# All of GpSimd's transfers kept in program order, and the token tiles of the mixer's second stage loaded two tiles ahead

## The chip, the cores and the metric

The kernel runs on one core of a Trainium2 chip. The core has five engines that run side by side, each with an in-order queue of its own: TensorE (PE in the profile, with its weight loads as PEld), VectorE (DVE), ScalarE (ACT), GpSimd (POOL) and SyncE (SP, which here only issues transfers). Transfers between HBM and on-chip memory are issued from an engine's queue and carried out by 16 DMA engines that all queues share. An engine waits for another, or for a transfer, through semaphores. The metric is the device time of one execution in microseconds, as the median over runs.

## The reference

The program has two halves that meet at the end. With `xn` the layer norm of the input `x` (2048 tokens by 512):

```
q = xn @ wq                        # 32 heads of 128
p = softmax(q k^T / sqrt(128))     # cached k, v: 32 heads x 2048 x 128
s = (p v) @ wo

h  = gelu(layernorm(xn) @ w1)      # 512 x 512
hs = shift(h) @ w2                 # four column groups, shifted by +1, -1, +2, -2 tokens
x1 = xn + hs
h2 = gelu(layernorm(x1) @ w3) @ w4 # 512 x 1792, 1792 x 512
g  = silu(x1 + h2)

out = x + s * g
```

The second half is called the mixer here. Inputs and output are bf16; sums are in fp32.

## The kernel before

The tokens are cut into 16 tiles of 128 (`t`), and into 4 groups of 512 (`qt`). The attention half is a sequence of 128 units: 8 groups of 4 heads, times 4 token groups, times 4 heads. A unit has 8 slots, 1024 slots in all. In each slot PE computes two blocks of scores (`ps_s`), ACT takes their exponential (`pT`, line 207), and PE multiplies an earlier slot's exponentials by the values (`ps_o`). VectorE adds up the exponentials (`acc`, lines 213 to 223).

The sums reach the normalisation by way of transfers on SP's queue: a transpose of `acc` (line 255), a sum and a reciprocal on VectorE (`sm`, `rc`, lines 260 and 245), a store of 2 KB to DRAM (`dr`, line 247), a broadcast load (`rb`, line 277), and then the product `oT = ps_o * rb` on VectorE (line 287). It reads a `ps_o` bank, of which there are two. The output projection collects four heads in `ps_wo`, and VectorE adds that to `s_acc` (line 361), after which the bank is free. The query projection of the unit after next (`ps_q`) uses the same bank.

The mixer's matmuls are pieces of work between these slots. A deque holds chunks, and each unit takes some five matmuls from it:

- Stage 1, `m1_chunk`: 16 chunks of 4 matmuls, GELU, result `hT`.
- Stage 2, `m2_chunk(t)`: 16 chunks of 4 matmuls, one per token tile, about 173 to 300 us. Tile `t` of the input is loaded as `xr` (`xn_load`, line 566), normalised in place on VectorE (`norm1`, line 411) when the chunk begins, and gets half of `ps_m` added (line 583). That is x1, which is stored to DRAM (`x1_d`, called `x_d` in the trace, line 585). Its statistics follow on VectorE (lines 589 and 590) and a reciprocal root on GpSimd (lines 127 and 128).
- Stage 3, `m3_chunk(c, fc)`: for each of 4 token groups (passes) 14 chunks of 4 matmuls with w3. `ln2` reloads four x1 tiles (`x1r`, line 613), normalises them eight slots later (line 620) and transposes them through SP (`xn2T`, line 623). The w3 weights come in pairs of chunks on GpSimd's queue (`w_sb`, line 657), each into one of two buffers when PE is done with it; w4 is loaded once (line 605).
- Stage 4, `m4_chunk(t)`: for each tile of the pass 14 matmuls with w4. x1 is loaded again as `xr` (line 667), `ps_m` is added (line 675), and after a tanh the gate `g` is stored to DRAM (`g_d`, lines 683 and 685).

In the last head group the output is made: for each tile `fin_load` loads `x` and `g` (`xl`, `gl`, lines 350 and 352), and `wo_out` computes the product and the sum (lines 366 and 368) and stores them (line 369). The last four tiles take another way, with loads on SP (`gf`, `xf`, lines 324 and 326).

Two pools of token tiles matter for the change: tag `tb` with 4 buffers holds `xr`, and tag `ta` with 6 buffers holds `x1r`, `xl` and `gl` (and earlier the input of the first layer norm).

What sets the order: nearly every instruction is wrapped in `pin`, which is `tc.keep_in_program_order`. Pinned instructions of an engine stay in the order in which the code writes them. An instruction that isn't pinned is placed by a scheduler, which can move it ahead of pinned ones on its engine's queue. Before the change these were free: `xl` and `gl`, the stage-2 store of x1, the reloads `x1r`, the stage-4 load of x1, and the store of `g`. All are transfers on GpSimd's queue. The loads of the w3 and w4 weights, of the stage-2 token tiles and GpSimd's arithmetic were pinned.

Of the kernel before, what the change touches and what calls it, by code (L numbers as in the profile page):

```python
# [11 lines left out]
BF16 = mybir.dt.bfloat16  # L12
# [5 lines left out]
def kernel(  # L18
# [15 lines left out]
    nc = tc.nc  # L34
    P = nc.NUM_PARTITIONS
# [3 lines left out]
    Sq, D = x2d.shape  # L39
# [4 lines left out]
    NT = Sq // P  # L44
# [18 lines left out]
    pin = tc.keep_in_program_order  # L63

    def pool(name, bufs=1, space=None, **kw):
        if space is not None:
            kw["space"] = space
        return tc.tile_pool(name=name, bufs=bufs, **kw)
# [16 lines left out]
        out=ident[:], in0=diag[:], scalar1=0.0, scalar2=None, op0=ALU.is_equal))  # L85
# [13 lines left out]
    tokp = ent(pool("tok", 4))  # L99
# [7 lines left out]
    xsrc = x2d.rearrange("(t p) d -> t p d", p=P)  # L107
    wq_v = A_wq.rearrange("(dc p) j -> p dc j", p=P)
    w3_v = B_w3.rearrange("(dc p) f -> p dc f", p=P)
    x1_d = [dsp.tile([P, D], BF16, name=f"x1_d{t}") for t in range(NT)]  # L110
    o_d = {qt: dsp.tile([P, HG, 512], BF16, name=f"o_d{qt}") for qt in range(QT)}
    g_d = [dsp.tile([P, D], BF16, name=f"g_d{t}") for t in range(NT)]
# [8 lines left out]
    def mm(out, lhsT, rhs, start, stop):  # L121
        mm_count[0] += out.shape[-1] / 512
        pin(nc.tensor.matmul(out=out, lhsT=lhsT, rhs=rhs, start=start, stop=stop))  # L123

    def rsqrt(out, var):
        ve = smp.tile([P, 1], FP32, name="ve")
        pin(nc.gpsimd.tensor_scalar(out=ve[:], in0=var, scalar1=EPS, scalar2=None, op0=ALU.add))
        pin(nc.gpsimd.tensor_tensor(out=out, in0=ve[:], in1=nhalf[:, 0:1], op=ALU.pow))
# [13 lines left out]
    def at(n, fn):  # L142
        todo[n].append(fn)

    def soft(n):
        while n % SPU not in (3, 5, 7):
            n += 1
        return n

    def evict(n):  # L150
        return n if n % SPU == SPU - 1 else n + 1
# [195 lines left out]

    def fin_load(t):
        xl = tokp.tile([P, D], BF16, tag="ta", bufs=6, name="xl")
        nc.gpsimd.dma_start(out=xl[:], in_=xsrc[t])  # L350
        gl = tokp.tile([P, D], BF16, tag="ta", bufs=6, name="gl")
        nc.gpsimd.dma_start(out=gl[:], in_=g_d[t][:])
        fin[t] = (xl, gl)

    def wo_post(g, t):
# [54 lines left out]
    def norm1(t, out, in_):  # L410
        pin(nc.vector.tensor_scalar(
            out=out, in0=in_, scalar1=mv1[t][:, 0:1], scalar2=rs1[t][:],
            op0=ALU.subtract, op1=ALU.mult))
# [70 lines left out]
    mlp = {}  # L484
# [70 lines left out]
    def m1_chunk(tt, jc):  # L555
        b = BASE_J[jc]
        jp = jc // 2
        return gelu_chunk(
            lambda dc: w1_sb[:, dc, jc * P:(jc + 1) * P],
            lambda dc: xnT[:, dc, tt * 512:(tt + 1) * 512],  # L560
            jc % 2, None,
            lambda: hT[:, 2 * jp:2 * jp + 2, b + tt * 512: b + (tt + 1) * 512])

    def xn_load(t):
        mlp["xnext"] = tokp.tile([P, D], BF16, tag="tb", bufs=4, name="xr")
        pin(nc.gpsimd.dma_start(out=mlp["xnext"][:], in_=xsrc[t]))

    def m2_chunk(t):
        def run(i, n):
            if i == 0:  # L570
                mlp["stage"] = 2
                mlp["ps"] = psX.tile([P, 512], FP32, tag="xm", name="ps_m")
                xr = mlp["xr"] = mlp.pop("xnext")
                at(n + 1 if n % SPU == 2 else n, lambda: norm1(t, xr[:], xr[:]))
                if t + 1 < NT:
                    xn_load(t + 1)
            c0 = BASE_J[i] + t * P - SHIFT[i]
            mm(mlp["ps"][:], hT[:, i, c0:c0 + P], w2_sb[:, i, :], i == 0, i == DC - 1)
            if i == DC - 1:
                ps, xr = mlp["ps"], mlp["xr"]  # L580

                def x1():
                    pin(nc.vector.scalar_tensor_tensor(
                        out=xr[:], in0=ps[:], scalar=0.5, in1=xr[:], op0=ALU.mult, op1=ALU.add))
                    nc.gpsimd.dma_start(out=x1_d[t][:], in_=xr[:])

                def stats():
                    bn = smp.tile([P, nc.vector.BN_STATS_DIM], FP32, name="bn")
                    pin(nc.vector.bn_stats(out=bn[:], in_=xr[:]))
                    pin(nc.vector.bn_aggr(out=mv2[:, t, :], in_=bn[:]))  # L590
                    rsqrt(rstd2[:, t:t + 1], mv2[:, t, 1:2])

                at(evict(n), x1)
                at(soft(n + 2), stats)
        run.size = DC
        return run
# [10 lines left out]
    def ln2(c, n):  # L607
        def start():
            mlp["xn2T"] = mp.tile([P, DC, 512], BF16, name="xn2T")
            xs = []  # L610
            for ts in range(4):
                xr = tokp.tile([P, D], BF16, tag="ta", bufs=6, name="x1r")
                nc.gpsimd.dma_start(out=xr[:], in_=x1_d[c * 4 + ts][:])
                xs.append(xr)
            mlp["xs"] = xs

        def apply(ts):
            t = c * 4 + ts
            xr = mlp["xs"][ts]
            pin(nc.vector.tensor_scalar(  # L620
                out=xr[:], in0=xr[:], scalar1=mv2[:, t, 0:1], scalar2=rstd2[:, t:t + 1],
                op0=ALU.subtract, op1=ALU.mult))
            pin(nc.sync.dma_start_transpose(
                out=mlp["xn2T"][:, :, ts * P:(ts + 1) * P], in_=xr[:]))

        at(n, start)
        for ts in range(4):
            at(soft(n + 8 + 2 * ts), lambda ts=ts: apply(ts))
# [31 lines left out]
    def m4_chunk(t):  # L660
        ts = t % 4

        def run(i, n):
            if i == 0:
                mlp["ps"] = psX.tile([P, 512], FP32, tag="xm", name="ps_m")
                mlp["xr"] = tokp.tile([P, D], BF16, tag="tb", bufs=4, name="xr")
                nc.gpsimd.dma_start(out=mlp["xr"][:], in_=x1_d[t][:])
            mm(mlp["ps"][:], mlp["h2"][i // 2][:, i % 2, ts * P:(ts + 1) * P],
               mlp["w4"][i][:], i == 0, i == FC - 1)
            if i == FC - 1:  # L670
                ps, xr = mlp["ps"], mlp["xr"]
                th = tokp.tile([P, D], BF16, tag="th", bufs=1, name="th")

                def x2():
                    pin(nc.vector.scalar_tensor_tensor(
                        out=xr[:], in0=ps[:], scalar=0.5, in1=xr[:], op0=ALU.mult, op1=ALU.add))

                def tanh(n):
                    pin(nc.scalar.activation(out=th[:], in_=xr[:], func=ACT.Tanh, scale=0.5))
                    at(soft(n + 2), silu)  # L680

                def silu():
                    pin(nc.vector.scalar_tensor_tensor(  # L683
                        out=xr[:], in0=th[:], scalar=1.0, in1=xr[:], op0=ALU.add, op1=ALU.mult))
                    nc.gpsimd.dma_start(out=g_d[t][:], in_=xr[:])  # L685

                at(evict(n), x2)
                at(n + 3, lambda: act_late.append(tanh))
        run.size = FC
        return run  # L690

    chunks = deque()
    hooks = {}
    for tt in range(QT):
        for jc in range(DC):
            chunks.append(m1_chunk(tt, jc))
    hooks[len(chunks) - 1] = lambda n: xn_load(0)
    for t in range(NT):
        if t == 8:
            hooks[len(chunks)] = lambda n: ln2(0, n)  # L700
# [78 lines left out]
    def normed(u):  # L779
        norm(u)  # L780
        gg, qq, hh = units[u]
        if hh == HG - 1 and (gg, qq) in deferred:
            pin(nc.sync.dma_start(out=o_d[qq][:], in_=oTs[(gg, qq)][:]))
        elif hh == HG - 1:
            wo_todo.extend((gg, 4 * qq + ts) for ts in range(4))
            if gg == NG - 1:
                fin_load(4 * qq)

    for n in range(NS):
# [46 lines left out]
        if p == 6 and wo_box:  # L836
            gg, t = wo_todo.popleft()
            wo_post(gg, t)
            if gg == NG - 1:
                at(n + 5, lambda t=t: wo_out(t))  # L840
                if t % 4 < 3:
                    fin_load(t + 1)
        if u == QUIET - 1 and p >= 6:
            wo_mm(*wo_todo[0], (0, 1) if p == 6 else (2, 3), "xm")
            if p == 7:
                gg, t = wo_todo.popleft()
# [47 lines left out]
    ts = [4 * LQ + j for j in range(4)]  # L894
# [75 lines left out]
```

## Time and profile before

| | us |
|---|---|
| median of 3 runs | 1255.7 (1254.87, 1255.70, 1258.52) |
| the profiled execution | 1254.97 |
| its span in the trace | 1253.2 |
| PE busy in the span | 1236.1 |
| ACT busy | 1129.9 |
| DVE busy | 1107.3 |
| POOL busy | 139.4 |

"Busy" leaves out instructions that only issue transfers on SP, set registers or wait. The span is what the trace covers; the rest of the profiled execution's time lies around it. In lists of waits a row names the engine that waited, its instruction, whom it waited for, the total, the number and the longest. In a timeline each row has the start, the duration, the engine, the line, the operation, the tile written and the tiles read, and in brackets the idle time before it and who ended it. PE's own durations overlap, as matmuls are pipelined: the distance of two starts is the better measure there. Some matmul records are missing in the trace.

The times of transfers from issue to landing, as medians in the view of transfers: `xr` from the input 2.4 us, `x1r` 3.5, `xr` from x1 2.6, `xl` 3.9, `gl` 2.9 (all 128 KB), w3's `w_sb` 3.8 (256 KB), `rb` 4.0 (256 KB), `dr` 1.7 (2 KB). The mean rate over the span is 101 GB/s, that of the fastest of the 40 slices 181. In 240 to 300 us the 16 transfer engines were busy for 0.62 of the time, in 405 to 450 for 0.59, in 620 to 665 for 0.67 and in 840 to 885 for 0.45.

### The profile page before, as it was taken

The page shows a single profiled execution, that of the slowest core. Times are in us where ns is not written, and L with a number is a line of the kernel's source. Part 1 is how long each engine was busy: PE and PEld are TensorE (multiplying, and loading weights), DVE is VectorE, ACT ScalarE, POOL GpSimd, SP SyncE. Part 2 cuts the span into 40 slices and gives each one's busy share as a digit, 9 for nine tenths or more (in the row PEclk, how much of TensorE's full clock was granted, in tenths as well). Part 3 has the DMA queues.
Part 4 walks back from the last instruction along what each step waited for, and adds up shares of the span by engine and source line. Part 5 has one row for each costly group of instructions (what it writes and reads, how often), then busy time and mean ns, then how long its engine had stood idle before and what let it go on. Part 6 is the DMA issues. An engine that isn't in the chain of part 4 may idle for free.

```text
span 1253.2 us, 16467 instructions
## 1 busy us (share of the span) xinstructions
PE 1236.1 (99%) x5757; PEld 597.9 (48%) x5872; DVE 1107.3 (88%) x1509; ACT 1129.9 (90%) x1285; POOL 139.4 (11%) x239
## 2 busy tenths in 40 slices
PE   8999999999999999999999999999999999999998
PEld 5444444444444444444444444444444444444444
DVE  7999999989899988889988889898888899888887
ACT  8999998888999888899988889998888999998893
POOL 4410013343101000000000000000000000000111
PEclk9999999999999999999999999999999999999999
DMA  9654453475635555344564345544446343552532
GB/s 181 140 111 93 79 111 89 115 151 135 129 75 112 108 101 104 62 96 90 103 120 72 77 101 97 106 72 100 99 89 114 67 81 81 117 116 55 151 77 68
DMA packets 235108, 126.70 MB, mean 101 GB/s; under 512 B 186832, under 2 KB 212048, under 8 KB 235024
## 3 DMA queue, kind: packets, MB, share of 16 engines
q1 hardware_dynamic: 225920, 100.40, 40.2%
q0 software_dynamic: 8672, 24.91, 7.9%
q8 instruction: 46, 0.75, 0.3%
q14 instruction: 38, 0.31, 0.1%
q10 hardware_dynamic: 432, 0.33, 0.1%
HBM read 82.58 MB, written 7.60 MB: 72 GB/s over the span
## 4 chain that ended last, share of the span: by engine, by line
PE 92%; DVE 3%; DMA 2%; ACT 1%; issue 1%; SPq 0%; POOL 0%; DVEq 0%; POOLq 0%
PE ps_o L123 33%; PE ps_s L123 33%; PE ps_m L123 9%; PE ps_q L123 8%; PE ps_wo L123 8%; ACT pT L207 1%; DVE acc L218 1%; DMA dr<-rc 1%; DMA xn2T<-x1r 0%; DVE oT L287 0%; DMA xr<-in_A_x_dram 0%; DMA vb<-in_A_v_cache_dram 0%; DVE acc L213 0%; SPq L158 0%; DMA rb<-dr 0%
## 5 line engine op out<-in xcount | busy, mean ns | idle before, releaser
L207 ACT ACTIVATE pT<-ps_s 128x1024 bf16<-128x1024 f32 x1024 | 1023.8, 1028 | 101.8 <-PE ps_s L123 87.4
L123 PE MATMUL ps_o<-pT,vb 128*128 128x512 bf16 x2014 | 600.6, 379 | 4.6 <-DVE oT L287 0.6
L123 PE MATMUL ps_s<-qT,kT 128*128 128x512 bf16 x1992 | 596.9, 379 | 2.3 <-ACT pT L207 0.5
L123 PEld LDWEIGHTS <-kT 128*128 128x128 bf16 x2048 | 231.0, 113 | 226.4 <-issue 4.9
L218 DVE TENSOR_TENSOR acc<-acc,pT 128x2048 bf16<-128x2048 bf16 x254 | 306.6, 1207 | 10.1 <-ACT pT L207 9.9
L123 PEld LDWEIGHTS <-vb 128*128 128x128 bf16 x2048 | 200.0, 98 | 226.6 <-issue 1.5
L213 DVE TENSOR_TENSOR acc<-pT 128x2048 bf16<-128x2048 bf16 x128 | 156.2, 1220 | 32.0 <-ACT pT L207 31.6
L123 PE MATMUL ps_q<-xnT,wq_h 128*128 128x512 bf16 (+1 forms) x516 | 151.0, 374 | 2.4 <-DVE s_acc L361 1.4
L123 PE MATMUL ps_wo<-wo_h,oT 128*128 128x512 bf16 (+1 forms) x470 | 138.8, 377 | 0.3
L287 DVE TENSOR_TENSOR oT<-ps_o,rb 128x512 bf16<-128x512 f32 x114 | 122.2, 1072 | 9.5 <-DMA rb<-dr 9.4
L361 DVE TENSOR_TENSOR s_acc<-ps_wo,s_acc 128x512 f32<-128x512 f32 x100 | 68.8, 688 | 43.8 <-PE ps_wo L123 42.9
L222 DVE TENSOR_TENSOR acc<-acc 128x1024 bf16<-128x1024 bf16 x127 | 86.8, 684 | 0.9
L193 DVE CAST qT<-ps_q 128x512 bf16<-128x512 f32 x109 | 75.0, 688 | 8.1 <-PE ps_q L123 7.4
L123 PEld LDWEIGHTS <-wq_h 128*128 128x128 bf16 x524 | 50.8, 98 | 62.5 <-issue 2.9
L260 DVE TENSOR_REDUCE sm<-accT 128x4 f32<-128x512 bf16 x114 | 77.5, 679 | 0.0
L123 PE MATMUL ps_m<-w_sb,h2T 128*128 128x512 bf16 x221 | 75.9, 379 | 0.1
L123 PE MATMUL ps_m<-xn2T,w_sb 128*128 128x512 bf16 x219 | 75.7, 379 | 0.1
L123 PEld LDWEIGHTS <-oT 128*128 128x128 bf16 x484 | 47.3, 98 | 56.5 <-DVE oT L294 0.6
L657 POOL DMA_DIRECT2D w_sb<-in_B_w_dram x28 | 21.1, 753 | 331.4 <-PE ps_m L123 273.5
L223 DVE TENSOR_TENSOR acc<-acc 128x512 bf16<-128x512 bf16 x127 | 54.0, 425 | 4.4
L685 POOL DMA_DIRECT2D g_d<-xr x16 | 8.8, 547 | 348.3 <-DVE xr L683 348.3
L496 DVE SCALAR_TENSOR_TENSOR sq<-sq,pre 128x1024 bf16<-128x1024 bf16 x36 | 44.0, 1222 | 4.0 <-ACT sq L492 4.0
(89 smaller groups left out, 599.8 us busy)
## 6 DMA issues: line engine op xcount, KB each, us to landing
rb<-dr SPq DMA_DIRECT2D x128, 256.0 KB, 4.0
vb<-in_A_v_cache_dram SPq DMA_DIRECT2D x64, 256.0 KB, 3.6
w_sb<-in_B_w_dram POOLq DMA_DIRECT2D x28, 256.0 KB, 3.8
wo_h<-in_A_wo_dram SPq DMA_DIRECT2D x32, 128.0 KB, 2.9
wq_h<-in_A_wq_dram SPq DMA_DIRECT2D x28, 128.0 KB, 2.9
kT<-in_A_k_cache_dram SPq DMA_TRANSPOSE x128, 3.4
dr<-rc SPq DMA_DIRECT2D x128, 2.0 KB, 1.7
xr<-in_A_x_dram POOLq DMA_DIRECT2D x16, 128.0 KB, 2.4
```

Source lines behind the costliest of these rows:

```text
L123: pin(nc.tensor.matmul(out=out, lhsT=lhsT, rhs=rhs, start=start, stop=stop))
L193: pin(nc.vector.tensor_copy(out=qT[:], in_=st[u].pop("psq")[:]))
L207: pin(nc.scalar.activation(out=s["pT"][-1][:, jj:jj + 2, :], in_=sps[:], func=ACT.Exp, scale=SCALE))
L213: pin(nc.vector.tensor_tensor(out=s["acc"][:], in0=s["pT"][0][:], in1=s["pT"][1][:], op=ALU.add))
L218: pin(nc.vector.tensor_tensor(out=a[:], in0=a[:], in1=st[u]["pT"][i][:], op=ALU.add))
L222: pin(nc.vector.tensor_tensor(out=a[:, 0:2, :], in0=a[:, 0:2, :], in1=a[:, 2:4, :], op=ALU.add))
L223: pin(nc.vector.tensor_tensor(out=a[:, 0, :], in0=a[:, 0, :], in1=a[:, 1, :], op=ALU.add))
L260: pin(nc.vector.tensor_reduce(out=sm[:], in_=s.pop("at")[:], axis=mybir.AxisListType.X, op=ALU.add))
L287: pin(nc.vector.tensor_tensor(out=oTs[(g, qt)][:, hh, :].rearrange(f, j=4), in0=s["o"].rearrange(f, j=4), in1=s["rb"].rearrange("x (p j) - ...
L361: pin(nc.vector.tensor_tensor(out=sa, in0=ps[:], in1=sa, op=ALU.add))
L496: pin(nc.vector.scalar_tensor_tensor(out=sq[:].rearrange(f2), in0=sq[:].rearrange(f2), scalar=1.0, in1=pre[:].rearrange(f2), op0=ALU.add, ...
L657: pin(nc.gpsimd.dma_start(out=w[:], in_=w3_v[:, :, fc * P:(fc + 2) * P]))
```

## The change

Two things are changed. First, the free transfers on GpSimd's queue are pinned: all of that queue is now in the order of the code. Second, the stage-2 token tiles are loaded two tiles ahead rather than one: a deque `xq` takes the place of the single name `xnext`, two tiles are loaded before the stage begins, and chunk `t` loads tile `t + 2`.

```
@@ fin_load
-        nc.gpsimd.dma_start(out=xl[:], in_=xsrc[t])
+        pin(nc.gpsimd.dma_start(out=xl[:], in_=xsrc[t]))
-        nc.gpsimd.dma_start(out=gl[:], in_=g_d[t][:])
+        pin(nc.gpsimd.dma_start(out=gl[:], in_=g_d[t][:]))
@@ xn_load
+    xq = deque()
     def xn_load(t):
-        mlp["xnext"] = tokp.tile([P, D], BF16, tag="tb", bufs=4, name="xr")
-        pin(nc.gpsimd.dma_start(out=mlp["xnext"][:], in_=xsrc[t]))
+        xq.append(tokp.tile([P, D], BF16, tag="tb", bufs=4, name="xr"))
+        pin(nc.gpsimd.dma_start(out=xq[-1][:], in_=xsrc[t]))
@@ m2_chunk
-                xr = mlp["xr"] = mlp.pop("xnext")
+                xr = mlp["xr"] = xq.popleft()
                 at(n + 1 if n % SPU == 2 else n, lambda: norm1(t, xr[:], xr[:]))
-                if t + 1 < NT:
-                    xn_load(t + 1)
+                if t + 2 < NT:
+                    xn_load(t + 2)
...
-                    nc.gpsimd.dma_start(out=x1_d[t][:], in_=xr[:])
+                    pin(nc.gpsimd.dma_start(out=x1_d[t][:], in_=xr[:]))
@@ ln2, start
-                nc.gpsimd.dma_start(out=xr[:], in_=x1_d[c * 4 + ts][:])
+                pin(nc.gpsimd.dma_start(out=xr[:], in_=x1_d[c * 4 + ts][:]))
@@ m4_chunk
-                nc.gpsimd.dma_start(out=mlp["xr"][:], in_=x1_d[t][:])
+                pin(nc.gpsimd.dma_start(out=mlp["xr"][:], in_=x1_d[t][:]))
...
-                    nc.gpsimd.dma_start(out=g_d[t][:], in_=xr[:])
+                    pin(nc.gpsimd.dma_start(out=g_d[t][:], in_=xr[:]))
@@ the list of chunks
-    hooks[len(chunks) - 1] = lambda n: xn_load(0)
+    hooks[len(chunks) - 1] = lambda n: [xn_load(t) for t in range(2)]
```

## The prediction

> **What bounds the kernel now.** I read the page's busy shares and 40 slices first, then PE's waits, then the timeline where PE stood still, then the transfers' times.
>
> ```profile
> PE 1236.1 (99%) x5757; PEld 597.9 (48%) x5872; DVE 1107.3 (88%) x1509; ACT 1129.9 (90%) x1285; POOL 139.4 (11%) x239
> PE   8999999999999999999999999999999999999998
> ```
>
> TensorE is full from end to end, at a mean granted clock of 0.999. Inside the steady work a 512-column matmul starts every 0.216 us (pairs 0.43 apart). So only time in which PE stands still can be won, and GpSimd (POOL), whose queue this change reorders, is at 11%. The list of PE's waits says how much that is:
>
> ```profile
> engine line waited for: us in total, times, longest us
> PE ps_q L123 <- DVE s_acc L361: 1.4, 1, 1.4
> PE ps_s L123 <- DVE ident L84: 1.4, 1, 1.4
> PE ps_o L123 <- DVE oT L287: 0.6, 2, 0.4
> ```
>
> The `ident` row is the start of the program. The first row and half of the third are one event. The timeline from 258 to 277 us shows it (start, duration, engine, line, what; in brackets the idle time before and who ended it):
>
> ```profile
> 258.22 0.55 POOL L613 DMA_DIRECT2D x1r<-x_d  x1 [3.25 <-DVE x1r L620]
> ...
> 260.18 0.54 POOL L585 DMA_DIRECT2D x_d<-xr  x1 [1.41 <-DVE xr L583]
> ...
> 265.82 0.55 POOL L613 DMA_DIRECT2D x1r<-x_d  x1 [5.10 <-DMA xn2T<-x1r]
> ...
> 267.69 0.62 POOL L566 DMA_DIRECT2D xr<-in_A_x_dram  x1
> ...
> 271.70 0.41 DVE L411 TENSOR_SCALAR xr<-xr,mv,rs 128x512 bf16<-128x512 bf16 x1 [3.13 <-DMA xr<-in_A_x_dram]
> 271.85 0.59 PE L123 MATMUL ps_o<-pT,vb 128*128 128x512 bf16 x2
> ...
> 273.90 0.59 PE L123 MATMUL ps_q<-xnT,wq_h 128*128 128x512 bf16 x2 [1.45 <-DVE s_acc L361]
> ...
> 275.49 1.05 DVE L287 TENSOR_TENSOR oT<-ps_o,rb 128x512 bf16<-128x512 f32 x1
> ...
> 276.60 0.59 PE L123 MATMUL ps_o<-pT,vb 128*128 128x512 bf16 x2 [0.38 <-DVE oT L287]
> ```
>
> The reader is to see a chain over four engines. An x1 reload (L613), which the scheduler had moved far ahead, sits on POOL's in-order queue and waits 5.10 us for a buffer that a transposing DMA still reads. Behind it stands the load of token tile 12 (L566, 267.69), only one tile ahead of its use. VectorE's normalisation L411 waits 3.13 us for that load, and everything behind it on VectorE is late: L361, which frees the bank that the next `ps_q` needs, and then L287, which frees a `ps_o`. PE's gaps: 271.85 to 273.90 is 2.05 us for two matmuls of 0.216, so 1.62 us lost; 275.62 to 276.60 is 0.98, so 0.55 lost. Together 2.17 us.
>
> Two smaller losses I found by the same sum over PE's starts: 0.41 us before 442.12 (L287 waited 2.66 us for its `rb`) and 0.37 us around 655 to 657 (L287 had waited 1.38 us). After the first 100 us PE loses nothing else: 2.95 us in all.
>
> **The change part by part.**
>
> *No instruction is added or removed.* In the two programs' instruction lists PE, ACT, DVE and SP have the same instructions in the same order; only POOL's order differs. POOL's transfers cost 0.54 to 0.63 us of its time each (0.75 for w3), as before.
>
> *Token loads two ahead (L566), the stage-2 x1 stores (L585) in order.* In the new POOL order the load of tile 12 stands after the store of tile 9 and its two small rsqrt operations, some 252 us, with no reload before it that waits for a buffer. With the median 2.4 us of its row it lands by 255, 16 us before L411 wants it. Of the four `tb` buffers a load takes the one of four tiles earlier, whose store is two tiles old. Nothing is late next on that path: the other 15 L411 show no wait even with loads one tile ahead. Worth: minus 2.17 us.
>
> *The x1 reloads (L613) in order.* They no longer float one by one into stages 2 and 4, but go in four groups of four, where the code writes them: the first at about 234 us, the others behind the last w3 load of a pass (405.26, 624.09, 842.90), each with a token or x1 load before and after. Six issues take 3.3 us. The first consumers (L620) stood at 246.96, 418.83, 637.80 and 857.13, over 9 us later, and x1r lands in 3.5 us. With six buffers and groups of four, the buffers they reuse were freed a pass earlier. Cost on VectorE: 0.
>
> *What queues behind a group is SP's softmax chain `dr`, `rb`,* on the same transfer engines (1.7 and 4.0 us median), which L287 waits for. This price the trace does not show, so I bound it. The group with w3 is 1.05 MB (the first one 0.79 MB, no w3). Suppose `dr` cannot move before the group has drained. At 181 GB/s (the fastest slice) that takes 5.8 us, at the mean 101 GB/s 10.4 us (first group 4.3 and 7.8). Then L287 is late, for the groups in order of time, by 0.9, 0, 2.5, 0 us at the fast rate and by 4.4, 2.2, 7.1, 1.6 at the mean one. Example, third group: 624.09 + 10.4 + 1.7 + 4.0 = 640.2 against L287 at 633.13. How much of that reaches PE: L287 late by 1.71 us (877.68) cost PE nothing, by 2.66 us cost 0.41, so about 2.25 us are absorbed. PE would lose 0.25 us at the fast rate, 2.15 + 4.85 = 7.0 at the slow one. In the other direction, two of the floated reloads went out at 431.43 and 434.05, in the middle of the 2.66 us wait, and two at 644 to 646, before the 1.38 us wait. With them gone up to 0.78 us may come back. I take 0, between minus 0.78 and plus 7.0: the nearest row, the tile load at 267.69 with 512 KB of w3 behind it and V and K loads around it, landed in 3.9 us against 2.4, so a burst costs a small transfer 1.5 us, inside the slack.
>
> [...]
>
> *x1 loads for the residual (L667).* The first four of them had floated to 285 to 306 us; now each is at its chunk's first matmul, 14 matmuls (some 27 us) before L675. A load may stand behind a store of `g_d` that waits for L683, which comes about 10 us after L675 of the tile before, leaving 15 us for a 2.6 us load. Cost 0; without that cover L675 would wait up to 2.6 us each.
>
> *The gate's store and loads (L685, L350, L352).* The first three tiles' loads no longer float to 651, 861 and 869. The tightest is tile 3: its loads stand behind the last store of `g_d` (1170.48), so they issue at about 1171.0 and 1171.6 and land by 1175.5 (3.9 us row), against L366 at 1179.13. SP's load of that `g_d` sees the store at the same time as before. Cost 0, with 3.6 us of slack; if that cover is gone, L366 waits and the tail moves by the excess.
>
> *Sum:* minus 2.17 us. The profiled execution took 1254.97 us (span 1253.2 plus 1.8 around it), so 1252.8 for the like of it. It lies 0.7 us below the median of the runs, 1255.7; from the median: **1253.5 us**, minus 0.17%.
>
> **The rivals.**
>
> A. *Bursts delay the softmax chain (slower).* Place: L287 after each reload group, worst at 633 us. Price at the mean rate: plus 7.0, net plus 4.8, 1260.5 us. It ends above the 0.3% bound when the groups take PE more than 5.9 us, that is when small transfers really wait for a drain at about 100 GB/s. For it: L287 already waits for `rb` eight times (9.4 us), and the slices around the second and third group are busier than average. Against it: transfer engines are 40 to 67% busy in those stretches, and even at the fastest slice's rate PE loses a quarter of a microsecond. [...]
>
> B. *The stall moves.* VectorE no longer waits at 271.70, but some L287 or L361 comes 3 us late elsewhere, as PE has no reserve and all phases shift by 2 us: 1255.7 us. For it: three L287 waits between 1.4 and 2.7 us stand near the threshold. Against: two of the three are next to reloads that leave.
>
> C. *The change doesn't do what it says:* tile 12's load is still late because POOL is held by a store that waits for VectorE (132.0 us of such waits in all). Then nothing is won: 1255.7. Against: the load stands one whole tile, some 9 us, earlier in the queue.
>
> D. *More comes back:* the stalls at 442 and 655 go too, 2.17 + 0.78 = 2.95, so 1252.7. More than 2.95 us is not there to win on PE.
>
> **How the numbers follow.** A measurement of this kernel can tell about 0.3% (3.8 us) from no change; the three runs lie 3.65 us apart. Forecast with D: 0.66; B 0.16; C 0.06; A 0.12. The gain of 2.2 to 3.0 us is below 3.8, so "faster" needs the scatter of the runs too: a third of 0.66, 0.22. Same: 0.44 of the forecast, 0.16 of B, 0.04 of C, 0.64 in all. Slower: A with 0.12 and 0.02 from C's scatter, 0.14. The range starts at 1250.8 (D and 1.9 us, half of the runs' spread) and ends at 1258.8, inside which all of B and C and the milder half of A lie.
>
> **What would show it.** Right: L411 without a wait on `xr`; no PE gap of over 0.5 us between 235 and 310 us; POOL without waits on `xn2T<-x1r`; x1 reloads in groups of four. Step by step wrong: L620, L675 or L366 waiting for a DMA (a moved load too late); L287's waits on `rb` grown well above 9.4 us near 242, 419, 633 and 857 with PE waiting on L287 (rival A); a PE wait on L361 or L287 elsewhere (B); L411 still waiting (C). What would make the forecast wrong as a whole is a transfer on POOL's queue that something on PE's path needs sooner than I read from the lists.

## The result and the profile after

| | before | after |
|---|---|---|
| median of 15 runs each | 1257.05 us (1253.94 to 1259.85) | 1253.82 us (1253.10 to 1256.44) |
| the profiled execution | 1254.97 | 1253.69 |
| its span | 1253.2 | 1251.9 |

The ratio is 0.9977, with a 95% interval of 0.9968 to 0.9985: the change saves 2.9 us, between 1.9 and 4.0. That is real, and smaller than the 0.3% that the prediction took as the bound of what counts. The two profiled executions are only 1.3 us apart; why the medians are further apart is taken up below. Two single runs in the comparisons below, one of 7560 us and one of 2206 us, were in a slow state and count in no median or ratio.

The page of the kernel after, its busy shares and PE's slices. A slice is 31 us long, so a stall of 2 us shows in neither row of slices, before or after; the lists further down are where the change is seen. (PE's busy time is larger than before by 6.7 us because the trace of before lacks 115 matmul records, 5757 against 5872, and not because there is more work.)

```profile
PE 1242.8 (99%) x5872; PEld 599.1 (48%) x5872; DVE 1107.5 (88%) x1509; ACT 1130.6 (90%) x1285; POOL 139.5 (11%) x239
PE   9999999999999999999999999999999999999998
```

The list of PE's waits of the kernel after. The rows on L361 (1.4 us) and on L287 (0.6 us) are gone. What is left are the start of the program, where `ident` and `xnT` belong, and waits of 0.4 us and less, most of them in the first 60 us and at the end.

```profile
PE ps_s L123 <- DVE ident L84: 1.4, 1, 1.4
PE ps_q L123 <- ACT xnT L459: 0.6, 2, 0.4
PE ps_s L123 <- ACT pT L207: 0.5, 2, 0.3
PE ps_s L123 <- DVE oT L294: 0.4, 1, 0.4
```

The timeline of the kernel after around the old stall (start, duration, engine, line, what). Lines of the second stage have moved by two: L566 is L568, L613 is L615.

```profile
236.01 2.12 POOL L615 DMA_DIRECT2D x1r<-x_d  x4
...
253.40 0.63 POOL L568 DMA_DIRECT2D xr<-in_A_x_dram  x1
...
269.57 0.40 DVE L411 TENSOR_SCALAR xr<-xr,mv,rs 128x512 bf16<-128x512 bf16 x1
...
272.94 0.59 PE L123 MATMUL ps_o<-pT,vb 128*128 128x512 bf16 x2
...
273.37 0.59 PE L123 MATMUL ps_q<-xnT,wq_h 128*128 128x512 bf16 x2
...
273.80 0.59 PE L123 MATMUL ps_s<-qT,kT 128*128 128x512 bf16 x2
```

The four x1 reloads of the first pass go out together at 236.01. The load of token tile 12 goes out at 253.40, 14 us earlier than before, and L411 at 269.57 has no bracket: it waits for nothing. `ps_o` and `ps_q`, which stood 2.05 us apart before, are 0.43 apart. A sum over PE's starts finds one gap between 70 and 1170 us, of 0.22 us at 95 us, which every trace of this study has and which is left out of the counts below. So the two small losses at 442 and around 655 us are gone as well, and with them all 2.95 us of losses that the prediction counted.

That the span shrank by only 1.3 us comes from outside that stretch. PE stood still 0.42, 0.41 and 0.16 us between 48 and 57 us, before the first transfer that the change moves, and 0.57 us at 1242. At the same early matmul the trace of after is already 1.1 us behind that of before. Gaps before 60 us come and go in all traces of this study, in kernels with and without the change, and count as scatter here. The gap near the end doesn't: eight of the nine traces of kernels with all transfers pinned have one there, of 0.19 to 0.57 us, and none of the five traces in which the output loads are free has one. In the trace of after L294 waits for its `rb` there. So the order of the output loads may cost a few tenths of a microsecond at the end; no run changes it alone, and the cause stays open.

VectorE's waits for transfers in the kernel after:

```profile
DVE oT L287 <- DMA rb<-dr: 8.9, 12, 1.8
DVE oT L294 <- DMA rb<-dr: 7.4, 7, 2.7
```

The waits for the broadcast `rb` at L287 were 9.4 us in 8 pieces with a longest of 2.7 before, and those at L294 5.1 us. Together they have grown by 1.8 us, the one on L411 (3.1 us) is gone, and no stage-3, stage-4 or output load (L622, L677, L366) shows up in the list. GpSimd no longer waits on `xn2T<-x1r`.

### The profile page after: what moved, and what is told of

The parts are those of the page before. It is cut to its first block, busy times and chain, and to the rows that moved or that the text cites. A ratio compares the mean times of both kernels' runs of the same rounds, so it can differ in the third digit from the quotient of the medians.

```text
span 1251.9 us, 16586 instructions
## 1 busy us (share of the span) xinstructions
PE 1242.8 (99%) x5872; PEld 599.1 (48%) x5872; DVE 1107.5 (88%) x1509; ACT 1130.6 (90%) x1285; POOL 139.5 (11%) x239
## 4 chain that ended last, share of the span: by engine, by line
PE 96%; DMA 1%; ACT 1%; DVE 1%; issue 0%; SPq 0%; POOL 0%; POOLq 0%; DVEq 0%
PE ps_s L123 35%; PE ps_o L123 34%; PE ps_m L123 10%; PE ps_q L123 9%; PE ps_wo L123 8%; ACT pT L207 1%; DMA dr<-rc 1%; DMA w_sb<-in_B_w_dram 0%; DMA rb<-dr 0%; PE ps_sum L123 0%; DVE gf L338 0%; DVE xf L343 0%; ACT pre L528 0%; DVE qT L193 0%; DVE bn L384 0%
## 5 line engine op out<-in xcount | busy, mean ns | idle before, releaser
L123 PE MATMUL ps_s<-qT,kT 128*128 128x512 bf16 x2048 | 608.9, 379 | 0.9 <-ACT pT L207 0.5
L123 PE MATMUL ps_o<-pT,vb 128*128 128x512 bf16 x2048 | 608.0, 379 | 0.3 <-DVE oT L294 0.3
L287 DVE TENSOR_TENSOR oT<-ps_o,rb 128x512 bf16<-128x512 f32 x114 | 122.3, 1073 | 8.9 <-DMA rb<-dr 8.9
L361 DVE TENSOR_TENSOR s_acc<-ps_wo,s_acc 128x512 f32<-128x512 f32 x100 | 68.7, 687 | 43.5 <-PE ps_wo L123 43.2
```

Of the source, the lines that this page charges most:

```text
L287: pin(nc.vector.tensor_tensor(out=oTs[(g, qt)][:, hh, :].rearrange(f, j=4), in0=s["o"].rearrange(f, j=4), in1=s["rb"].rearrange("x (p j) - ...
L361: pin(nc.vector.tensor_tensor(out=sa, in0=ps[:], in1=sa, op=ALU.add))
```

## The experiments

**The theory.** One x1 reload that waits for its buffer at the head of GpSimd's queue delays the load behind it; VectorE waits for that load, and PE for VectorE. **The rivals:** that it is the earlier token load, and not the pinned queue, that does the work; that other moved transfers give or cost something; and that groups of reloads take a part of the gain back by delaying the softmax chain `dr`, `rb`. The runs also had to say why the median moved by more than the trace did.

### Each half alone

The first four kernels ran on one chip, with before at a median of 1257.52 us (19 runs).

**Only the second half**, tiles loaded two ahead, with the other transfers free as before:

```
-                if t + 1 < NT:
-                    xn_load(t + 1)
+                if t + 2 < NT:
+                    xn_load(t + 2)
```

with the deque and the two first loads as in the change.

> The kernel before with the second half of the change alone: token tiles loaded two ahead, no further transfer pinned. Theory 1 (the loss at 271 to 277 us is that of tile 12's load behind a reload that waits for a buffer; either half of the change cures it): L411 does not wait for xr, the PE gaps of 1.62 and 0.55 us near 272 to 277 are gone, but POOL still waits some 5 us on xn2T<-x1r, and the small gaps near 442 and 655 us stay. Ratio to before 0.9983, some 2.2 us. Rival (the order of GpSimd's queue is what counts, one tile or two is the same): ratio 1.000, L411 still waits about 3 us.

Measured: 1255.44 us (10 runs), ratio 0.9983 (0.9972 to 0.9993). L411 doesn't wait and the stall at 272 us is gone. The list of POOL's waits shows that the blocked reload is still there:

```profile
POOL x1r L615 <- DMA xn2T<-x1r: 10.3, 5, 5.6
```

The blocked queue has lost its victim, but there is other harm. The timeline of the same kernel, where SPq is SP's queue of transfers:

```profile
274.97 0.34 SPq L247 DMA_DIRECT2D dr<-rc  x1
...
280.55 0.34 SPq L277 DMA_DIRECT2D rb<-dr  x1
...
284.78 1.06 DVE L287 TENSOR_TENSOR oT<-ps_o,rb 128x512 bf16<-128x512 f32 x1 [2.31 <-DMA rb<-dr]
...
285.89 0.59 PE L123 MATMUL ps_o<-pT,vb 128*128 128x512 bf16 x2 [1.12 <-DVE oT L287]
```

From `dr` to `rb` took 5.6 us among other loads, against a median of 1.7 us from issue to landing in the trace of before. L287 waited 2.31 us and PE stood still for 1.29 us. Another 0.37 us went before 291.87 and 0.62 us before 442.48; the small loss around 655 us, which was expected to stay, isn't there. The same late `rb` comes back at the end of this section in a kernel whose reloads are all in order and whose queue is held by other work (`dr` at 276.27, `rb` at 281.47). What the two share is a queue that, once free, sends token tiles and 512 KB of w3 weights shortly before `dr`. That this delays `dr` is argued from the order of the rows and not shown by a run of its own. This half removes the large stall and leaves smaller ones.

**Only the first half**: the six transfers pinned as in the change, tiles still loaded one ahead.

> The kernel before with the first half of the change alone: all of GpSimd's transfers pinned, token tiles still one ahead. Theory 1: POOL does not wait on xn2T<-x1r any more, tile 12's load issues in time, L411 does not wait, the gaps at 272 to 277 are gone, and so are those at 442 and 655 us, since no reload floats there: ratio 0.9977, as the whole change. Rival (two tiles ahead is what does it): L411 still waits for xr somewhere in 235 to 310 us, ratio 0.999 to 1.000.

Measured: 1252.98 us (1252.66 to 1253.64, 5 runs), ratio 0.9966 (0.9954 to 0.9979). Tile 12's load goes out at 262.32 us, still one tile ahead of its use; L411 at 269.04 doesn't wait; PE has no gap between 70 and 1170 us but that at 95 us. In order, one tile ahead is early enough.

**One line of the first half**: only the x1 reloads pinned.

```
-                nc.gpsimd.dma_start(out=xr[:], in_=x1_d[c * 4 + ts][:])
+                pin(nc.gpsimd.dma_start(out=xr[:], in_=x1_d[c * 4 + ts][:]))
```

> The kernel before with one line pinned, the x1 reloads of each pass (L613). Theory 1 (these reloads alone did the harm): POOL's waits on xn2T<-x1r are gone, L411 does not wait, no PE gap over 0.5 us between 235 and 310 us, ratio 0.9977 to 0.9983. Rival (the other floating transfers, of the residual and of the output, cost as much): a gain of less than half, ratio 0.999 or more.

Measured: 1253.09 us (1252.88 to 1254.20, 5 runs), ratio 0.9968 (0.9955 to 0.9981), again with no other PE gap between 70 and 1170 us. This one line does all that the times can tell of the change. Pinning the other free transfers as well (stores of x1 and of the gate, loads of the residual and the output) changes nothing that shows in the times.

**The whole change once more**, for the comparison on this chip.

> The changed kernel once more, for a second trace and the comparison on the same chip. Theory 1: no PE gap between 70 and 1170 us, ratio 0.9977 within 0.001. What the small gaps at 48 to 57 us and at 1242 us in its first trace are is open: if they are scatter of single transfers they stand elsewhere or are missing here; if the change makes them, they are there again, 0.3 to 0.6 us each.

Measured: 1253.63 us (1252.90 to 1254.32, 9 runs), ratio 0.9971 (0.9961 to 0.9981). The two kernels with pins alone are some 0.6 us lower, but the intervals overlap, and the traces differ only at the ends: after's second trace lost 1.07 and 0.46 us before 60 us, and nothing else between 70 and 1170. Whether the loads two tiles ahead cost half a microsecond is not settled; they gain nothing here.

### The kernel before, looked at again

The saving (2.9 to 4.3 us by the ratios so far) was more than the 2.2 us that the trace of before showed at its stall. So I looked at two further executions of the unchanged kernel.

> The kernel before, a second trace. The median of its runs lies 3 to 4 us above that of the changed kernel, but the first trace shows 2.95 us of PE gaps after 70 us. Theory 1: the chain from the waiting reload over tile 12's load to L411 is there again with 1.5 to 3 us of PE gaps near 270 us, and gaps at L287 elsewhere come and go with single transfers, 2 to 5 us in all. Rival (the gap near 270 us is scatter of one trace): L411 does not wait here, and the gaps stand at other places.

> The kernel before, a third trace, with the same expectations: by theory 1 the gap near 270 us again, 2 to 5 us of PE gaps after 70 us in all; by the rival none near 270 us.

Measured: 1257.88 and 1257.40 us, both well above the 1254.97 of the first trace. The same chain is worse in both. The timeline of the second of them:

```profile
267.18 0.55 POOL L613 DMA_DIRECT2D x1r<-x_d  x1 [5.52 <-DMA xn2T<-x1r]
...
269.08 0.62 POOL L566 DMA_DIRECT2D xr<-in_A_x_dram  x1
...
273.76 0.41 DVE L411 TENSOR_SCALAR xr<-xr,mv,rs 128x512 bf16<-128x512 bf16 x1 [4.25 <-DMA xr<-in_A_x_dram]
...
275.96 0.80 PE L123 MATMUL ps_q<-xnT,wq_h 128*128 128x512 bf16 x2 [2.59 <-DVE s_acc L361]
...
276.55 1.06 PE L123 MATMUL ps_s<-qT,kT 128*128 128x512 bf16 x2
...
277.40 1.06 PE L123 MATMUL ps_o<-pT,vb 128*128 128x512 bf16 x2
```

The reload waited 5.52 us, not 5.10. Tile 12's load took 4.7 us from issue to L411, not 4.0, and L411 waited 4.25 us, not 3.13 (3.95 in the other execution). PE's gap is 2.76 us. And then something new: pairs of matmuls that start 0.43 us apart everywhere else start 0.85 apart. The windows view of the same execution (start and end, length, busy time and count of PE, PEld, DVE, ACT and POOL, then the granted clock, the transfer engines' share and GB/s; a packet counts whole in the window in which it starts, so that the share can pass 1) shows why:

```profile
269.38:272.79 3.41, 3.41 (x18) 1.62 (x17) 0.12 (x1) 2.94 (x3) 3.30 (x7) 1.00 0.90 172
272.79:276.20 3.41, 0.82 (x5) 0.30 (x4) 2.44 (x4) 1.15 (x2) 0.45 (x1) 1.00 1.08 202
276.20:279.62 3.42, 3.42 (x10) 1.23 (x9) 3.39 (x6) 1.29 (x2) 1.19 (x2) 0.50 1.21 279
279.62:283.03 3.41, 3.41 (x17) 1.62 (x16) 3.31 (x7) 3.25 (x4) 0.32 (x2) 1.00 0.30 61
```

After the stall TensorE's granted clock stood at 0.50 from 276.20 to 279.62 us. To follow the cost: from the `ps_o` ahead of the gap to the `ps_o` six pairs later takes 2.59 us at full pace. It took 4.75 us in the first trace (271.85 to 276.60), so 2.2 us were lost; 7.03 here (272.77 to 279.80), so 4.4 lost; and in the other execution 6.38 (273.20 to 279.58) with 0.34 more in the next pair, so 4.1 lost. The first trace was the mild one of three.

### Would groups of reloads hurt?

Rival A of the prediction said that a group of transfers on GpSimd's queue delays `dr` and `rb`. To find where this begins, each reload of a group was followed by extra copies of 128 KB from DRAM to DRAM, which nobody reads: one per reload (the group grows from about 1.05 to 1.6 MB), or three (2.6 MB).

```
+                for e in range(1):      # 3 in the second kernel
+                    pin(nc.gpsimd.dma_start(out=j_d[4 * c + 1 * ts + e][:], in_=xsrc[4 * c + ts]))
```

> The changed kernel with each group of four x1 reloads joined by four more transfers of 128 KB on the same queue (copies in DRAM that nothing uses), so a group with w3 moves some 1.6 MB. Theory 1 (small transfers take turns with a burst and keep their slack): L287's waits on rb grow by at most 2 us at each of the four places, PE loses under 0.5 us, ratio to before 0.997 to 0.998. Rival A (a small transfer waits until the group has drained): at 181 GB/s the third group lasts 8.7 us, L287 is some 5 us late there and PE loses about 3 us; ratio 0.999 to 1.001.

Measured: 1255.21 us (1253.73 to 1256.92), ratio to before 0.9986 (0.9976 to 0.9995), with before at 1257.24 (17 runs). L288 (L287 moved by a line) waits 8.3 us for `rb` in all, no more than without the extra copies. PE loses 0.26, 0.18 and 0.27 us, about 0.7 us together. By the ratios that is 1 to 2 us above the change alone (0.9971 and 0.9977), with intervals that overlap; the trace explains 0.7.

> The same with twelve more transfers of 128 KB to each group, some 2.6 MB with w3. Theory 1: the issue alone takes 16 times 0.55 us, 9 us; dr and rb at most double while it lasts, so L287 is late by 2 to 4 us at two or three places and PE loses 0 to 3 us; ratio 0.997 to 1.000. Rival A: groups last 14 us at 181 GB/s, L287 is late by over 8 us at the third group and over 4 us at the others, PE loses 10 us or more; ratio 1.005 or more.

Measured: 1262.72 us (1258.99 to 1264.77), ratio 1.0034 (1.0020 to 1.0048), slower than before. VectorE's waits for `rb` at this line have more than doubled, to 19.3 us, and PE loses about 8 us after the first 70, some 6 of them right behind such a wait. Neither expectation was met: the theory allowed PE 3 us at most, the rival began at 10. The timeline of this kernel at the third group:

```profile
628.22 0.32 SPq L248 DMA_DIRECT2D dr<-rc  x1
...
634.42 0.32 SPq L278 DMA_DIRECT2D rb<-dr  x1
...
639.93 1.05 DVE L288 TENSOR_TENSOR oT<-ps_o,rb 128x512 bf16<-128x512 f32 x1 [4.50 <-DMA rb<-dr]
...
641.03 0.59 PE L124 MATMUL ps_o<-pT,vb 128*128 128x512 bf16 x2 [2.28 <-DVE oT L288]
```

`dr` is 2 KB and took 6.2 us to its next step; L288 waited 4.50 us and PE stood still for 2.45. So a large group does delay the softmax chain, at the place that the prediction named, but it decides only with a group two and a half times as large as that of the change. It isn't a drain of the whole group, as rival A supposed: the group's transfers are issued from 626.31 to 637.32, and `rb`, which reads what `dr` has stored, goes out at 634.42, before the last of them.

### The late load by itself

The last four kernels make tile 12's load late by work, not by a blocked reload. GpSimd's queue gets so many extra operations (an `iota` into a tile that nobody reads any more, 0.307 us each) ahead of that load. They separate three questions: is a late load alone enough; what decides whether the clock drops; and does loading two tiles ahead protect?

```
+        for _ in range(24 if t == 12 else 0):   # 24, 21 or 19; t == 13 with two tiles ahead
+            pin(nc.gpsimd.iota(diag[:], pattern=[[-1, P]], base=0, channel_multiplier=1,
+                               allow_small_or_imprecise_dtypes=True))
```

The first three are built on the kernel with pins alone.

> The kernel with all pins and one tile ahead (label pins), with 24 small GpSimd operations (an iota of 128 by 128 each) put ahead of tile 12's load, so that only this load and what follows it on POOL's queue come later. It measures the disputed cost by itself. Theory 2 (the loss near 270 us is PE's gap alone while the gap is short; a gap of over some 2.4 us also brings the half clock for 3.4 us and another 1.7 us, as in the second and third trace of before): with the 24 operations taking 6 to 8 us L411 waits 1 to 4 us; PE's gap is that less about 1 us; if it stays under 1.7 us the clock stays at 1.00 and the run is 0.5 to 2.2 us above that of pins; if it passes 2.4 us the clock falls to 0.50 for 3.4 us and the run is 4 us above. Rival (the half clock in those two traces had another cause than the gap): the clock does not follow the gap's length, and the run is above pins by the gap alone.

Measured: 1258.06 us (1256.97 to 1260.36), ratio 1.0007 (0.9996 to 1.0018), with before at 1257.38 (12 runs). 7.36 us of work on an engine that is 11% busy takes back the whole gain: by the ratios 5 us more than pins alone. L411 waited 4.67 us, PE's gap was 3.13 us, and the clock was at half for 3.41 us after it. The timeline:

```profile
262.25 7.36 POOL L566 IOTA diag<- 128x128 f32 x24
...
269.88 0.63 POOL L569 DMA_DIRECT2D xr<-in_A_x_dram  x1 [0.26 <-issue]
...
273.71 0.41 DVE L411 TENSOR_SCALAR xr<-xr,mv,rs 128x512 bf16<-128x512 bf16 x1 [4.67 <-DMA xr<-in_A_x_dram]
...
275.91 0.91 PE L123 MATMUL ps_q<-xnT,wq_h 128*128 128x512 bf16 x2 [2.97 <-DVE s_acc L361]
```

No reload waits in this kernel, so the late load alone makes the stall.

> As hold24, with 19 operations. They took 0.307 us each there, so tile 12's load is 1.5 us earlier: L411 waits 3.1 us, PE's gap is 1.6 us, as in the first trace of before. Theory 2: the granted clock stays at 1.00, and the run is some 1.6 us above pins and 3.2 us below hold24 (1.5 us less gap and 1.7 us less for the half clock). Rival (no jump, cost goes with the gap alone): 1.5 us below hold24.

Measured: 1256.86 us (1254.96 to 1258.22), ratio 0.9998 (0.9987 to 1.0010), with before at 1256.71. The load was issued 1.5 us earlier against the rest of its trace, as meant, but it took 4.9 us from issue to L411 and not 3.8, so L411 waited 4.21 us instead of about 3.1 and PE's gap was 2.70. The granted clock was at 0.50 from 276.26 to 279.67 us.

> As hold24, with 21 operations: L411 waits 3.75 us, PE's gap is 2.2 us, between the 1.62 that left the clock alone and the 2.45 that did not. Theory 2: either the one or the other, in steps, with some runs near hold19 plus 0.6 us and some 1.7 us above that, if the limit lies here. Rival: all runs 0.9 us below hold24.

Measured: 1257.69 us (1256.33 to 1260.53), ratio 1.0007 (0.9996 to 1.0017). L411 waited 4.25 us, and PE's gap was 2.75 us, slightly longer than with 19 operations. The granted clock stayed at 1.00 (270 to 282 us). I had expected the length of the gap to decide; these two traces say that it doesn't decide alone. What else they show is in the last section. The median is the longer of the two all the same: it mixes runs with and without a drop (by the count of the last section at least 4 of 10 have one here, and at least 2 of 10 with 19 operations).

The fourth is the whole change, with 24 operations at the same place, where they now delay the load of tile 13.

> The changed kernel with the same 24 operations at the same place of POOL's queue (chunk 11), which with two tiles ahead stand in front of tile 13's load. Theory 1 (two tiles ahead is insurance on top of the pins: nothing in the present order, but a cover for 7.4 us of delay): L411 does not wait, no gap near 270 us, ratio to before 0.997 as without the operations. Rival (the delay reaches PE another way, as POOL's stores, w3 loads and rsqrt are late too): a gap somewhere in 262 to 310 us.

Measured: 1254.51 us (1253.45 to 1256.37), ratio 0.9983 (0.9973 to 0.9994). The timeline of this kernel:

```profile
263.78 7.37 POOL L568 IOTA diag<- 128x128 f32 x24
...
270.50 0.49 DVE L411 TENSOR_SCALAR xr<-xr,mv,rs 128x512 bf16<-128x512 bf16 x1
...
271.41 0.63 POOL L571 DMA_DIRECT2D xr<-in_A_x_dram  x1 [0.26 <-issue]
```

The delayed load goes out at 271.41, and L411 at 270.50 already has its tile. PE has no gap near 270 us, but 0.42 and 0.37 us at 286 and 292, in the stretch that the rival named. The delay that cost 5 us with loads one tile ahead costs about 1 us with two (0.9983 against 0.9971 and 0.9977 without it, with intervals that overlap). So the second half of the change is an insurance: worth nothing measurable once the reloads are in order, and some 3 to 4 us when something else holds GpSimd.

## Why the prediction was right, and where it wasn't

It said 1253.5 us in a range of 1250.8 to 1258.8, most likely "the same" by its bound of 0.3%. The median was 1253.82 and the saving 0.23%. The chain that it named is the cause; that the time came within 0.4 us is in part luck, as follows.

**The chain over four engines: right, and shown.** A late load alone makes the stall, without any blocked reload; with the reloads pinned the load is early and L411 doesn't wait.

**"Token loads two ahead ... Worth: minus 2.17 us": the credit was put on the wrong half.** The load was at 253.40, close to the 252 us that the order gave. But the prediction counted the stall's removal under this part and the pinned reloads at zero to 0.78. The runs show that either half removes the stall, and that pinning one line is enough for all that the times show. The reason was in the prediction's own profile lines: with the reload out of the way, the queue had no cause to be late.

**The size of that term: low.** 2.17 us was right for the one trace it was read from (gaps of 1.62 and 0.55). In two other executions the same stall cost 4.1 and 4.4 us, since the load landed later against PE and the clock stood at 0.50 for 3.42 us afterwards. The sentence "more than 2.95 us is not there to win on PE" holds for that execution and not for the kernel. By their ratios the kernels with pins alone were 4.3 and 4.0 us under before, and the change itself 2.9 and 3.6. The predicted time still came close because it was set from a median of three runs, 1255.7, that lies 1 to 2 us below the medians of 12 to 25 runs (1256.7 to 1257.5) in the later comparisons: a gain that was too small, taken from a start that was too low.

**x1 reloads in groups, taken at 0: right for the time, with two readings that don't hold.** L287 waited 0.98 us at the third group (632.71) and PE didn't. The bound by draining at 101 GB/s would have had it 7.1 us late. The packets of that place show no drain: `dr`, issued at 624.78, has its 128 packets between 626.26 and 628.64, and of the group's 256 packets 124 start before them, 115 among them and 17 after. But "a burst costs a small transfer 1.5 us" was too little for `dr`: from it to the next step took 4.4 us there, against a median of 1.7, while `rb` beside the group of the change took 3.5 us, less than its median of 4.0. Nor does any run show that `dr` at most doubles while a group lasts, which the expectation for 2.6 MB counted with: it took 6.2 us in that kernel.

Nor do "about 2.25 us" of lateness vanish everywhere. Around 440 us waits at L287 of up to 2.09 us cost PE nothing and one of 2.66 us cost 0.41; but at 285 us 1.41 us cost 0.42 and 2.31 us cost 1.29, so some 1.0 us is covered there. The prediction's own 1.38 us near 655, followed by 0.37 us of loss, pointed to that.

**Rival D, "more comes back": the gain came, its cause is open.** The stalls at 442 and 655 us are gone in the traces of the change. But the third trace of before has neither, the second has 0.14 us at 445 and 0.22 at 882, and the kernel with all pins and 21 operations has 0.21 at 444. They come and go, and that the free reloads make them isn't shown.

**Rival A (slower): not at this size.** It needs groups of 1.6 MB for a first loss of under 1 us on PE and 2.6 MB for 8.

**Rivals B and C: not seen.** No stall of the kind came back between 70 and 1170 us, and the load was not late. Rival B's picture, a new wait at L287 soon after the old stall, is what the second half alone does (1.29 us at 285.89).

**Residual loads, output loads and gate stores at 0: right.** No wait on them in the list of after, and pinning them on top of the reloads changed nothing that the times show. The gap of a few tenths of a microsecond near the end, seen only with the output loads pinned, is the one thing that may belong to them.

## What to carry to other kernels

On an in-order queue that also carries loads for the critical path, look for transfers that a scheduler may move and that have to wait for a buffer: one pinned line in the right place did here what a whole queue in order and a deeper prefetch did together. Before sizing a stall from one trace, look at a second and a third execution, since a wait of 3 to 4 us lost 2 or more than 4 us here according to what the granted clock did after it (1.00 or 0.50 for 3.42 us). A load one step deeper cost nothing that could be measured here and took most of the harm out of a delay of 7 us that nobody planned.

## What the runs showed of the hardware that was not expected

**After four stalls of TensorE, of 2.45 to 3.13 us, its granted clock stood at 0.50 for 3.41 or 3.42 us; after three others, of 1.62, 2.45 and 2.75 us, it stayed at 1.00.** The four stretches at half begin at 276.83 (before, second), 276.20 (before, third), 276.02 (pins, 24 operations) and 276.26 us (pins, 19 operations), and after each the clock was full again. The clock's record has such a stretch at the end of the program too: in the first trace of before it says full for 1245.865 us, from 4.6 to 1250.5, and in that of after for 1242.451 us, from 7.0 to 1249.4, and then half. The two lengths differ by 3.414 us, as long as one stretch at half, and are 365 and 364 steps of 3.413. From this I estimate, and no run was set up to show it, that the clock changed in these executions on a grid of such steps from the start of its record, at 4.6 and 7.0 us in these two; a stall then falls differently into the grid from one execution to the next. The windows of 3.41 us around the stalls were these. They end where the clock fell; where it didn't, their bounds are counted in steps of 3.413 us and are part of that estimate:

| trace | PE busy in the 3.41 us window of the stall | clock in the next window |
|---|---|---|
| pins, 24 operations | 0.44 | 0.50 |
| before, third | 0.82 | 0.50 |
| before, second | 1.13 | 0.50 |
| pins, 19 operations | 1.32 | 0.50 |
| before, first | 1.91 | 1.00 |
| pins, 21 operations | 2.09, then 2.15 | 1.00 |
| bursts of 2.6 MB, at 641 us | 2.24, then 2.30 | 1.00 |

The two kernels with 19 and 21 operations, whose gaps are 2.70 and 2.75 us long, are the closest pair. The windows of the first:

```profile
272.84:276.26 3.42, 1.32 (x7) 0.52 (x5) 1.76 (x3) 1.90 (x2) 0.81 (x2) 1.00 1.04 167
276.26:279.67 3.41, 2.97 (x8) 1.01 (x8) 3.41 (x5) 1.02 (x1) 0.99 (x2) 0.50 1.12 250
```

and of the second, where the estimated bound at 274.97 cuts the gap in two:

```profile
271.56:274.97 3.41, 2.09 (x10) 0.91 (x9) 0.94 (x2) 2.66 (x3) 2.16 (x5) 1.00 1.05 248
274.97:278.39 3.42, 2.15 (x10) 1.03 (x10) 3.42 (x5) 1.09 (x2) 0.18 (x1) 1.00 1.32 254
```

So in these stalls the half clock followed windows with 0.44 to 1.32 us of work on PE, and not those with 1.91 to 2.30. The end of the program agrees: there the clock fell after windows with 1.06 us of work (before, first, 1247.06 to 1250.48) and 0.87 us (after, 1245.97 to 1249.39). By estimate a drop costs about 1.7 us: half of 3.41, less what was idle in it.

This was read out of stalls and ends of traces, not set up as an experiment, and it doesn't show that the work in such a window is what decides. How much of the larger gain the drop explains can be judged from the mean granted clock of every run. A stretch of 3.41 us at half takes 0.0014 off it, and the half clock at the very end took 0.0011 off in the first trace of before (2.72 us of its span) and 0.0010 in that of after (2.51 us). By this estimate 0.998 or less means a drop in mid-program, 1.000 means none, and 0.999 leaves it open. Of 73 runs of before in the four later comparisons 18 show 0.998 or less, with a median of 1257.9 us, and 22 show 1.000, with a median of 1256.6; in each of the four the runs with a drop have the longer median. Of the 54 runs of the change, of the kernels with pins alone, with 1.6 MB and of the change with 24 operations none is below 0.999. So the drop is a part of the larger gain, but only a part: the runs of before without it still lie 2.8 us above the 1253.8 of the change, close to the 2.95 us that the first trace lost on PE. In the kernel with pins and 24 operations, moreover, the three runs at 1.000 (1258.07 to 1258.97 us) are no shorter than the others, which stays unexplained.
